# Attention pairs in rounds of two, with the first batch's result kept on chip and the weight decode spread over two rounds

## The chip, the core and the metric

The kernel runs on one NeuronCore of a Trainium2 chip. A core has a matrix engine (PE, TensorE), three elementwise engines (ACT, DVE, POOL), an engine that issues transfers (SP), an on-chip memory SBUF, and PSUM, the memory that PE writes its products to. Each engine works through its own list of instructions; semaphores make one wait for another. The metric is device time in microseconds: 791.69 as the median of three executions (791.29 to 794.2).

## The reference

Three stages follow one another over 4 batches, 448 positions and 768 channels (12 heads of 64):

```
# 1. attention with a sigmoid in place of the softmax
scores = q @ k.T / sqrt(64) - log(448)
x = sigmoid(scores) @ v                      # heads side by side: (4, 448, 768)
# 2. a gated projection
gate = sigmoid(causal depthwise convolution of x, 5 taps, conv_w)
x2 = (gate * (x @ w_val)) @ w_out
# 3. a mixer over positions, then one over channels
u = x2 + (relu(x2.T @ w_tok1) @ w_tok2).T
out = u + relu(u @ w_ch1) @ w_ch2            # hidden width 1536
```

The inputs of stages 2 and 3 need more accuracy than one fast product has, so each 128-channel operand is held as a high and a low part and multiplied three times. Weights arrive as 64-bit words.

## The kernel before

Work is laid out with channels on the partitions. Two heads make a *pair*, so there are 6 pairs per batch and 24 in all, numbered 0 to 23.

**A pair.** `load_qk` and `load_v` fetch q, k and v. `scores(i, c)` multiplies a chunk `c` of 128 keys by all queries for both heads into a PSUM tile `pss`, and `sigmoid` on ACT turns it into a tile `a`. The last 64 keys of two neighbouring pairs share one tile (`scores_last`, PSUM `psl`, SBUF `al`). `av` multiplies the three sigmoid tiles by v into `psy`; `av_last` adds the shared one for both pairs of two, and ACT copies the two results out of PSUM as `x`, which SP stores to a scratch tensor `xscr` in DRAM. `x_back` later loads it again with four zero columns in front (`xb`).

**Per pair, after attention.** `post_parts` computes the convolution `gate` on DVE (one multiply and four multiply-adds) and splits `xb` into `xs`, a high part by ACT and a low part by DVE. ACT's sigmoid over `gate` comes last.

**Decoding a weight.** `fetch` loads a block of 64-bit words into `raw` (three buffers). `decode_parts` gives four steps: `masks` (three DVE instructions), `rebase` (ACT), `low` (three DVE instructions, the last writes the low part) and `high` (ACT writes the high part). There are 18 blocks ahead of the channel mixer: six of `w_val`, six of `w_out`, four of `w_tok1` (`wt1`) and two of `w_tok2` (`wt2`).

**Dense work.** `dense_steps(b)` is a list of steps for one batch: 18 thirds of the `w_val` product (PSUM `psd`, from `xs`), whose results are multiplied by `gate` and split into `gv`, then the `w_out` product (`psd` from `gv`), copied out by ACT as `x2T`, transposed (`pst`), and the mixer over positions (`pst1`, `pst2`). `x2T` lies in a pool `late` that takes over the room of the decode pool `dec`, so its first write waits until the last decode is through.

**What sets the order.** `PLAN` (L25) says which pairs run beside which dense work. Its first two rows are written out by hand in `lead` (pairs 0 to 11, no dense work) and `lead_val` (three pairs beside the `w_val` product of batch 0), inside `manual_schedule`: engines take instructions as they are emitted. From then on a planner sets the order by its own costs; it may also put later instructions between those of the written part, as it does with the convolutions of batch 1. In `lead`, each pair is emitted as `av(i)`, then the scores of pair i+1. `DEC_LEAD` names the eight pairs beside which a block is decoded, `DEC_VAL` spreads seven more over the six half steps of `lead_val`, and the last three are decoded by `late()`. The convolutions of batch 0 start at pair 6 (`POST_FROM`). The channel mixer (`psh`, `pso`) at the end is one dense run of PE.

Of the kernel before, what the change touches and what calls it, by code (L numbers as in the profile page):

```python
# [33 lines left out]
DEC_LEAD = (0, 1, 2, 3, 4, 5, 8, 10)  # L34
DEC_VAL = (1, 1, 1, 1, 1, 2)
CONV_AT = 3

POST_FROM = 6
# [3 lines left out]
def tile_kernel(ctx, tc, qT, kT, v, w_val, conv_w, w_out, w_tok1, w_tok2, w_ch1, w_ch2, out):  # L42
# [63 lines left out]
    def decode_parts(pool, n, raw, h_out, l_out):  # L106
        w = raw[:, : 2 * n].rearrange("p (n t) -> p n t", t=2)
        lo, hi = w[:, :, 0], w[:, :, 1]
        e = raw[:, :n]
        t = {}  # L110

        def masks():
            a = pool.tile([P, DC], I32, tag="dec_a", bufs=2, name="dec_a")[:, :n]
            c = pool.tile([P, DC], I32, tag="dec_c", bufs=1, name="dec_c")[:, :n]
            t["a"], t["c"] = a, c
# [3 lines left out]
                out=c.bitcast(F32), in0=lo.bitcast(U32), scalar=2.0**-32, in1=c, op0=ALU.mult, op1=ALU.add  # L119
# [5 lines left out]
        def low():  # L125
            a, c = t["a"], t["c"]
# [5 lines left out]
                out=l_out, in0=c.bitcast(F32), scalar=2.0**-20, in1=e.bitcast(F32), op0=ALU.mult, op1=ALU.mult  # L132
            )

        def high():
            nc.scalar.activation(out=h_out, in_=t["a"].bitcast(F32), func=AF.Copy)  # L136
# [28 lines left out]
    def dec_conv(pool):  # L165
        n = KD * KW

        def go(raw):
            h = pool.tile([P, n], F32R, tag="cwHL", bufs=1, name="cwH")
            lo = pool.tile([P, n], F32R, tag="cwL", bufs=1, name="cwL")  # L170
            masks, rebase, low, high = decode_parts(pool, n, raw, h, lo)

            def total():
                high()
                nc.vector.tensor_tensor(out=cw, in0=f(h), in1=f(lo), op=ALU.add)

            return masks, rebase, low, total

        return (lambda raw: nc.gpsimd.dma_start(raw, conv_w.bitcast(I32))), go
# [55 lines left out]
    def sigmoid(ps, tag, bufs):  # L235
        a = attn.tile([P, 2, S], F32, tag=tag, bufs=bufs, name=tag)
# [3 lines left out]
    def scores(i, c):  # L240
# [5 lines left out]
        a_t[i, c] = sigmoid(ps, "a", A_BUFS)  # L246
# [22 lines left out]
    def av_last(i):  # L269
# [6 lines left out]
        for h in range(2):  # L276
            x = attn.tile([P, S], F32, tag="x", bufs=2, name="x")
            nc.scalar.activation(out=x, in_=y_t.pop(i + h)[:, :S], func=AF.Copy)
            nc.sync.dma_start(xscr[i + h], x)

    def step_av(i):
        av(i)
        if i % 2:
            av_last(i - 1)
            posts.extend((i - 1, i))
# [16 lines left out]
    def x_back(i):  # L302
        x = attn.tile([P, PAD + S], F32, tag="xb", bufs=2, name="xb")
# [4 lines left out]
    def post_parts(i):  # L308
# [6 lines left out]
        def first():  # L315
# [3 lines left out]
            split(xs[:, 0], xs[:, 1], x[:, PAD:])  # L319
# [5 lines left out]

        def last():
            nc.scalar.activation(out=acc, in_=acc, func=AF.Sigmoid)

        return first, last
# [8 lines left out]
    def dense_steps(b):  # L338
# [3 lines left out]
        def proj(sel, j, part):  # L342
# [16 lines left out]
            if sel == 0:  # L359
                g = gate_t.pop(b * NP + j)  # L360

                def gated():
                    nc.vector.tensor_tensor(out=g, in0=ps[:, :S], in1=g, op=ALU.mult)  # L363
                    gv[j] = mid.tile([P, 2, S], F32R, tag="g", bufs=6, name="gv")
                    split(gv[j][:, 0], gv[j][:, 1], g)

                if dn.get("hold") is None:
                    gated()
                else:
                    dn["hold"].append(gated)  # L370
# [93 lines left out]

    for i in range(2):
        load_qk(i)
    for i in range(2):
        load_v(i)
    load_vl(0)
    load_qk(2)  # L470
    make_identity(nc, ident)
    craw = dec.tile([P, 2 * KD * KW], I32, tag="craw", bufs=1, name="craw")
    cld, cgo = dec_conv(dec)
# [3 lines left out]
    back = 0  # L477
# [32 lines left out]

    def lead():
        nonlocal back
        after = []

        def dec_begin():
            raw, go = raws.pop(0)
            return go(raw)

        dec_load()
        for c in range(NF):  # L520
            scores(0, c)
        scores_last(0)
        dec_load()
        for i in pairs0:
            load_qk(i + 3)
            step_av(i)
            step_loads(i)
            for half in step_scores(i):
                for fn in half:
                    fn()  # L530
# [255 lines left out]
```

## Time and profile before

| | |
|---|---|
| median of three executions | 791.69 us |
| the profiled execution | 795.41 us, span 793.6 us |
| mean granted PE clock | 0.993 of full speed |
| busy: PE / DVE / ACT / POOL | 765.4 / 382.5 / 268.3 / 27.3 us |
| scores of a chunk, L245 (288 records) | 70.5 us, 590 ns mean |
| sigmoid of a chunk, L237 (72) | 69.1 us, 1004 ns mean |
| products with v, L266 (288 records) | 65.7 us, 552 ns mean |
| convolution tap, L321 (96) | 65.1 us, 682 ns mean |
| DMA moved | 80.49 MB, 101 GB/s over the span |

A profiled span of 793.6 us lies inside an execution of 795.41 us. PE is busy for 96% of the span, so what counts is where it is not, and where it is busy for longer than the same work needs elsewhere. In a timeline row the first number is the start, the second the time to the end of the last of `xN` instructions of one kind; records of PE overlap, so the time that a piece of work takes is read from its start to the start of the next piece. A bracket at the end of a row is the idle time before it and what ended it. Products of fp32 operands show two records per instruction.

### The profile page before, as it was taken

What the parts mean: (1) busy time and instruction counts of PE and PEld (TensorE: products, weight loads), DVE (VectorE), ACT (ScalarE), POOL (GpSimd) and SP (SyncE); (2) the same over time, 40 slices, a digit from 0 to 9 for tenths busy, and PEclk for the clock granted to TensorE, in tenths of its full rate; (3) what the DMA queues carried; (4) which work ended last, traced back from release to release, by engine and by line L of the source; (5) the groups of instructions that cost most, each with busy time, mean ns of one, the idle gap of its engine ahead of it and who ended that gap; (6) DMA issues with size and microseconds to landing.
All of it is one profiled execution on the core that took longest, in us unless ns stands there. A gap on an engine that the chain in (4) does not pass through costs nothing.

```text
span 793.6 us, 9619 instructions
## 1 busy us (share of the span) xinstructions
PE 765.4 (96%) x3776; PEld 605.2 (76%) x3776; DVE 382.5 (48%) x659; ACT 268.3 (34%) x404; POOL 27.3 (3%) x73
## 2 busy tenths in 40 slices
PE   7999899699999999999999999999999999999998
PEld 3333456576767777868998999889999999999997
DVE  2758789812583237246688799970002200120002
ACT  5888656523343324232343344430002000100000
POOL 0100001000000000001000000000000000000000
PEclk9999999899999999999999999999999999999999
DMA  8867544312221021014453445551001400050001
GB/s 283 286 231 240 187 149 128 98 33 95 67 84 48 22 72 36 12 47 138 131 191 115 151 163 161 167 192 48 0 1 59 152 1 0 8 190 1 0 1 70
DMA packets 50685, 80.49 MB, mean 101 GB/s; under 512 B 4544, under 2 KB 46032, under 8 KB 50640
## 3 DMA queue, kind: packets, MB, share of 16 engines
q1 hardware_dynamic: 47280, 65.29, 25.8%
q0 software_dynamic: 3360, 14.58, 5.4%
q8 instruction: 30, 0.49, 0.3%
q14 instruction: 15, 0.12, 0.0%
HBM read 63.34 MB, written 16.52 MB: 101 GB/s over the span
## 4 chain that ended last, share of the span: by engine, by line
PE 59%; issue 19%; DVE 12%; DMA 6%; ACT 2%; POOL 1%; SPq 0%; POOLq 0%; DVEq 0%; ACTq 0%
PE psh L675 18%; PE pso L691 18%; PE psd L353 8%; PE psy L266 5%; PE pss L245 5%; DVE gate L321 3%; PE pst L399 2%; DVE dec_a L127 2%; DMA raw<-w_ch 2%; PE pst L412 2%; DVE dec_c L118 2%; DMA k<-kT 1%; ACT a L237 1%; DVE wch L131 1%; DMA xb<-xscr 1%
## 5 line engine op out<-in xcount | busy, mean ns | idle before, releaser
L675 PE MATMUL psh<-us,wch 128*128 128x448 f32 x864 | 184.8, 366 | 0.8 <-ACT wch L136 0.7
L691 PE MATMUL pso<-r,wch 128*128 128x448 f32 x864 | 184.1, 366 | 0.6 <-ACT r L91 0.6
L675 PEld LDWEIGHTS psh<-us,wch 128*128 128x128 f32 x864 | 162.1, 188 | 15.9 <-ACT wch L136 1.7
L691 PEld LDWEIGHTS pso<-r,wch 128*128 128x128 f32 x864 | 162.1, 188 | 15.0 <-ACT r L91 1.0
L93 DVE SCALAR_TENSOR_TENSOR r<-psh,r 128x448 fp32r<-128x448 f32 x48 | 29.9, 624 | 210.3 <-ACT r L91 210.0
L91 ACT ACTIVATE r<-psh 128x448 fp32r<-128x448 f32 x48 | 26.1, 543 | 225.3 <-PE psh L675 225.0
L353 PE MATMUL psd<-gv,w 128*128 128x448 f32 x432 | 96.2, 376 | 1.8 <-DVE gate L363 1.2
L353 PEld LDWEIGHTS psd<-gv,w 128*128 128x128 f32 x432 | 81.1, 192 | 18.7 <-ACT x L384 4.8
L353 PE MATMUL psd<-xs,w 128*128 128x448 f32 x432 | 92.6, 369 | 1.4 <-DVE h L93 1.3
L353 PEld LDWEIGHTS psd<-xs,w 128*128 128x128 f32 x432 | 80.1, 188 | 16.3 <-issue 5.2
L237 ACT ACTIVATE a<-pss,bias_s 128x896 f32<-128x896 f32 x72 | 69.1, 1004 | 34.5 <-PE pss L245 34.2
L245 PE MATMUL pss<-q,k 64*128 64x448 f32 x288 | 70.5, 590 | 4.0 <-DMA k<-kT 4.0
L266 PE MATMUL psy<-a,v 128*64 128x448 f32 x288 | 65.7, 552 | 4.7 <-ACT a L237 4.5
L321 DVE SCALAR_TENSOR_TENSOR gate<-xb,cw,gate 128x448 f32<-128x448 f32 x96 | 65.1, 682 | 1.9
L123 ACT ACTIVATE dec_a<-dec_a,exp_b 128x768 int32<-128x768 int32 (+3 forms) x43 | 37.5, 872 | 59.0 <-DVE dec_a L116 54.4
L245 PEld LDWEIGHTS pss<-q,k 64*128 64x128 f32 x288 | 27.1, 195 | 38.7 <-issue 24.7
L266 PEld LDWEIGHTS psy<-a,v 128*64 128x64 f32 x288 | 18.4, 135 | 41.1 <-ACT a L237 24.0
L127 DVE SCALAR_TENSOR_TENSOR dec_a<-raw,dec_a 128x768 int32<-128x768 int32 (+2 forms) x42 | 37.3, 888 | 11.6 <-ACT dec_a L123 11.5
L118 DVE SCALAR_TENSOR_TENSOR dec_c<-raw,dec_c 128x768 f32<-128x768 uint32 (+2 forms) x42 | 37.4, 890 | 1.0
L374 DVE COPY x2T<-x2T 128x64 f32<-128x64 f32 x24 | 4.5, 192 | 62.8 <-ACT x2T L373 62.8
L116 DVE TENSOR_SCALAR dec_a<-raw 128x768 int32<-128x768 int32 (+2 forms) x42 | 21.9, 521 | 22.5 <-DMA raw<-w_val 13.0
L399 PE MATMUL pst<-x,wt1H 128*128 128x384 f32 x112 | 30.2, 338 | 0.5 <-DVE x L385 0.4
(68 smaller groups left out, 569.3 us busy)
## 6 DMA issues: line engine op xcount, KB each, us to landing
raw<-w_ch SPq DMA_DIRECT2D x24, 768.0 KB, 4.4
q<-qT SPq DMA_DIRECT2D x24, 224.0 KB, 3.3
k<-kT SPq DMA_DIRECT2D x24, 224.0 KB, 4.2
xscr<-x SPq DMA_DIRECT2D x24, 224.0 KB, 2.4
xb<-xscr SPq DMA_DIRECT2D x24, 224.0 KB, 2.6
uscr<-x2T POOLq DMA_DIRECT2D x24, 224.0 KB, 2.4
u<-uscr SPq DMA_DIRECT2D x24, 224.0 KB, 3.6
ur<-uscr SPq DMA_DIRECT2D x24, 224.0 KB, 3.5
```

Of the source, the lines that this page charges most:

```text
L93: nc.vector.scalar_tensor_tensor(out=l_out, in0=src, scalar=0.0, in1=f(h_out), op0=ALU.max, op1=ALU.subtract)
L118: nc.vector.scalar_tensor_tensor(out=c.bitcast(F32), in0=lo.bitcast(U32), scalar=2.0**-32, in1=c, op0=ALU.mult, op1=ALU.add)
L123: nc.scalar.activation(out=t["a"], in_=t["a"], func=AF.Relu, scale=8.0, bias=exp_b)
L127: nc.vector.scalar_tensor_tensor(out=a, in0=hi, scalar=-0x80000000, in1=a, op0=ALU.bitwise_and, op1=ALU.bitwise_or)
L237: nc.scalar.activation(out=a, in_=ps[:, :, :S], func=AF.Sigmoid, bias=bias_s, scale=QK_SCALE)
L245: nc.tensor.matmul(ps[:, j, :S], k[rows, c * P : (c + 1) * P], q[rows], start=True, stop=True)
L266: nc.tensor.matmul(y[cols, :S], vn[:, c, cols], a[:, j], start=c == 0, stop=False)
L321: nc.vector.scalar_tensor_tensor(out=acc, in0=x[:, t : t + S], scalar=cw[:, p * KW + t : p * KW + t + 1], in1=acc, op0=ALU.mult, op1=ALU.add,)
L353: nc.tensor.matmul(ps[:, :S], w(a, kk), s[:, c, :], start=kk == 0 and n == 0, stop=kk == KD - 1 and n == 2,)
L399: nc.tensor.matmul(ps[:, :HALF], a, x[:, m], start=n == 0, stop=n == len(mm) - 1)
L675: nc.tensor.matmul(ps[:, :S], wch[fc][:, 0, a, kk * P : (kk + 1) * P], us_t[b, kk][:, c, :], start=kk == 0 and n == 0, stop=kk == KD - 1 a ...
L691: nc.tensor.matmul(acc[j][:, :S], wch[fc][:, 1, a, j * P : (j + 1) * P], r[:, c, :], start=fc == 0 and n == 0, stop=fc == KF - 1 and n == 2,)
```

## The change

Four things are changed, all in front of the planner's part or in the tables it reads.

- `lead` goes in rounds of two pairs: both `av`, `av_last`, both copies, then all scores of the *next* two pairs. The sigmoid tiles of the round ahead lie in the six buffers of `g`, which `gv` uses later. A second copy out of PSUM is DVE's.
- x of batch 0 (pairs 0 to 5) is written into `xb` with its zero columns and stays there; `xscr` is used from pair 6 on. `xb` now has four buffers, which the copies and `x_back` share; the two buffers of `x` are gone.
- A block's `masks` are emitted one round (in `lead_val` one half step) ahead of its `low` and `high`; the round's `xs` parts and gates likewise follow one and two rounds behind the convolution. `masks` keeps its third result in `raw`, so that `dec_c` is free at once. The small block of `conv_w` is loaded first of all.
- `lead_val` runs beside four pairs (12 to 15), with all remaining ten blocks in `DEC_VAL`; later rows of `PLAN` move by one, and batch 2 runs beside two pairs.

```diff
 PLAN = (
     (None, "", range(0, 12)),
-    (0, "v", range(12, 15)),
-    (0, "o", range(15, 18)),
-    (1, "vo", range(18, 21)),
-    (2, "vo", range(21, 24)),
+    (0, "v", range(12, 16)),
+    (0, "o", range(16, 19)),
+    (1, "vo", range(19, 22)),
+    (2, "vo", range(22, 24)),
     (3, "v", ()),
 )
-DEC_LEAD = (0, 1, 2, 3, 4, 5, 8, 10)
-DEC_VAL = (1, 1, 1, 1, 1, 2)
+DEC_LEAD = (1, 1, 1, 1, 1, 2, 1)
+DEC_VAL = (1, 1, 1, 1, 1, 1, 2, 2)
...
+    def evict(i, on_vector=False, stays=False):
+        y = y_t.pop(i)[:, :S]
+        t = attn.tile([P, PAD + S], F32, tag="xb", bufs=4, name="xb")
+        x = t[:, PAD:]
+        if stays:
+            nc.vector.memset(t[:, :PAD], 0.0)
+            x_t[i] = t
+        if on_vector:
+            nc.vector.tensor_copy(x, y)
+        else:
+            nc.scalar.activation(out=x, in_=y, func=AF.Copy)
+        if not stays:
+            nc.sync.dma_start(xscr[i], x)
+            posts.append(i)
...
+    def dec_masks(n):
+        for _ in range(n):
+            raw, go = raws.pop(0)
+            begun.append((go(raw), True))
+            begun[-1][0][0]()
...
+        dec_masks(DEC_LEAD[0])
+        conved, gates = [], []
+        for n, p in enumerate(pairs0[::2]):
+            done = begun[:]
+            begun.clear()
+            for parts, _ in done:
+                parts[1]()
+            for parts in conved:
+                parts[1]()
+            for parts, _ in done:
+                parts[2]()
                 dec_load()
+            for parts in conved:
+                parts[2]()
+            for fn in gates:
+                fn()
+            for parts, _ in done:
+                parts[3]()
+            gates = [parts[3] for parts in conved]
+            dec_masks(DEC_LEAD[n + 1])
+            for i in (p, p + 1):
+                av(i)
+                load_v(i + 2)
+            av_last(p)
+            load_vl(p + 2)
+            for i in (p, p + 1):
+                evict(i, i > p, p < NP)
+            conved = [post_parts(i) for i in (p, p + 1)] if p < NP else []
+            scores_last(p + 2)
+            for i in (p + 2, p + 3):
+                for c in range(NF):
+                    if i <= pairs0[-1] + 1:
+                        scores(i, c, i <= pairs0[-1])
+                if i + 3 <= pairs0[-1] + 3:
+                    load_qk(i + 3)
+            for parts in conved:
+                parts[0]()
...
 # lead_val, one half step
                 for fn in steps[done:last]:
                     fn()
                 done = last
+                for parts in held:
+                    parts[0]()
+                for fn in subs:
+                    fn()
+                dec_low()
+                dec_masks(DEC_VAL[at])
+                for fn in gates:
+                    fn()
+                for parts in held:
+                    parts[1]()
+                dec_act()
```

PE in the lead, before, over two pairs (`psy` the products with v, `psl` and `pss` the scores):

```order
L266 MATMUL psy<-a,v 64x448 x6
L245 MATMUL pss<-q,k 128x448 x6
L266 MATMUL psy<-a,v 64x448 x6
L275 MATMUL psy<-al,vl 64x448 x4
L256 MATMUL psl<-q,k 64x448 x4
L245 MATMUL pss<-q,k 128x448 x6
```

And one round of the change:

```order
L261 MATMUL psy<-ga,v 64x448 x12
L270 MATMUL psy<-al,vl 64x448 x4
L251 MATMUL psl<-q,k 64x448 x4
L240 MATMUL pss<-q,k 128x448 x12
L261 MATMUL psy<-ga,v 64x448 x12
```

The same instructions stand in fewer, longer blocks: every product with v now has the scores of a whole round between its sigmoid and itself.

ACT in the change, the fourth round, from the end of the third round's sigmoids (`dec_a` is a block's rebase, `w0_3_0` its high part, `xs` and `gate` those of batch 0, `xb` the copy out of PSUM):

```order
L119 ACTIVATE dec_a_438<-dec_a_438,exp_b_66 128x768
L333 ACTIVATE xs_474<-xb_468 128x448
L333 ACTIVATE xs_476<-xb_471 128x448
L339 ACTIVATE gate_366<-gate_366 128x448
L339 ACTIVATE gate_368<-gate_368 128x448
L136 ACTIVATE w0_3_0_98<-dec_a_438 128x768
L282 ACTIVATE xb_577<-psy_552 128x448
L232 ACTIVATE al_588<-psl_583,bias_s_62 128x896
L232 ACTIVATE ga_593<-pss_590,bias_s_62 128x896
```

Six instructions stand between the last sigmoid of one round and the copy that opens the next.

DVE in the change near the end of `lead_val` (`raw_1041` and `raw_1075` are the last two blocks of `w_tok1`, `xb_1256` is x of pair 6 come back from DRAM, `gate_475` and `gv_1062` belong to the projection of batch 0):

```order
L114 SCALAR_TENSOR_TENSOR raw_1041<-raw_1041,dec_c_1144 128x256
L323 TENSOR_SCALAR gate_1263<-xb_1256,cw_69 128x448
L327 SCALAR_TENSOR_TENSOR gate_1263<-xb_1256,cw_69,gate_1263 128x448
L336 TENSOR_TENSOR xs_1262<-xb_1256,xs_1262 128x448
L327 SCALAR_TENSOR_TENSOR gate_1263<-xb_1256,cw_69,gate_1263 128x448
L112 TENSOR_SCALAR dec_a_1148<-raw_1075 128x256
L113 TENSOR_SCALAR dec_c_1149<-raw_1075 128x256
L327 SCALAR_TENSOR_TENSOR gate_1263<-xb_1256,cw_69,gate_1263 128x448
L114 SCALAR_TENSOR_TENSOR raw_1075<-raw_1075,dec_c_1149 128x256
L377 TENSOR_TENSOR gate_475<-psd_1063,gate_475 128x448
```

The planner has put the convolution of pair 6 (batch 1) in front of the last decodes and of the gated products; before, such convolutions stood among the last decodes too. Counted from the first of these `xb_1256` rows, `gv_1135`, the fifth of six `gv`, is the 33rd DVE instruction, and the last row of `wt2` the 43rd.

SP at the same place (`xscr<-xb` stores a pair, `xb<-xscr` loads one back):

```order
L209 DMA k<-kT 128x448
L284 DMA xscr<-xb 128x448
L312 DMA xb<-xscr 128x448
L284 DMA xscr<-xb 128x448
L218 DMA v<-v 128x3x128
L224 DMA vl<-v 64x128 x2
L312 DMA xb<-xscr 128x448 x3
```

The first load of batch 1 stands behind the store of pair 14, which waits for ACT's copy of that pair.

## Rows read from the trace of the kernel before

**Rows 1.** Timeline of PE, two pairs of the lead: start us, us, what.
```profile
9.27 2.48 PE L266 MATMUL psy<-a,v 128*64 128x448 f32 x12
...
16.57 0.98 PE L275 MATMUL psy<-al,vl 64*64 64x448 f32 x8
17.37 0.93 PE L256 MATMUL psl<-q,k 64*64 64x448 f32 x8
18.23 2.53 PE L245 MATMUL pss<-q,k 64*128 64x448 f32 x12
20.69 2.50 PE L266 MATMUL psy<-a,v 128*64 128x448 f32 x12
```

**Rows 2.** Timeline of PE, end of the lead and a projection.
```profile
81.71 0.97 PE L256 MATMUL psl<-q,k 64*64 64x448 f32 x4 [1.91 <-DMA k<-kT]
82.61 4.22 PE L245 MATMUL pss<-q,k 64*128 64x448 f32 x12
88.00 2.48 PE L266 MATMUL psy<-a,v 128*64 128x448 f32 x12 [1.17 <-ACT a L237]
...
96.89 3.91 PE L353 MATMUL psd<-xs,w 128*128 128x448 f32 x18
```

**Rows 3.** Timeline of PE, start of the w_out product.
```profile
141.77 1.77 PE L245 MATMUL pss<-q,k 64*128 64x448 f32 x8
149.80 1.09 PE L382 MATMUL pst<-ident,x2T 128*128 128x128 f32 x4 [6.26 <-issue]
150.54 5.77 PE L353 MATMUL psd<-gv,w 128*128 128x448 f32 x18
```

**Rows 4.** Timeline of DVE and of ACT at the same place.
```profile
143.13 0.68 DVE L321 SCALAR_TENSOR_TENSOR gate<-xb,cw,gate 128x448 f32<-128x448 f32 x1
...
148.38 0.62 DVE L131 SCALAR_TENSOR_TENSOR wt2L<-dec_c,raw 128x448 fp32r<-128x448 f32 x1
...
149.16 0.98 ACT L373 ACTIVATE x2T<-psd 128x448 f32<-128x448 f32 x2 [0.75 <-DVE wt2L L131]
```

**Rows 5.** Windows: length, busy us (instructions) by engine, PE clock, DMA, GB/s.
```profile
80.00:90.00 10.00, 7.12 (x28) 2.69 (x28) 6.05 (x11) 6.75 (x10) 0.73 (x2) 0.83 0.87 292
```

**Rows 6.** Timeline of ACT in the lead.
```profile
65.37 0.94 ACT L123 ACTIVATE dec_a<-dec_a,exp_b 128x768 int32<-128x768 int32 x1
66.21 0.56 ACT L327 ACTIVATE gate<-gate 128x448 f32<-128x448 f32 x1
...
67.65 0.98 ACT L278 ACTIVATE x<-psy 128x448 f32<-128x448 f32 x2 [0.41 <-PE psy L275]
...
69.43 2.80 ACT L237 ACTIVATE a<-pss,bias_s 128x896 f32<-128x896 f32 x3
```

**Rows 7.** Timeline of DVE in the lead: a decode, then a convolution.
```profile
64.78 0.55 DVE L116 TENSOR_SCALAR dec_a<-raw 128x768 int32<-128x768 int32 x1
...
66.72 0.97 DVE L127 SCALAR_TENSOR_TENSOR dec_a<-raw,dec_a 128x768 int32<-128x768 int32 x1
...
69.20 0.45 DVE L316 TENSOR_SCALAR gate<-xb,cw 128x448 f32<-128x448 f32 x1
69.56 0.62 DVE L97 TENSOR_TENSOR xs<-xb,xs 128x448 fp32r<-128x448 f32 x1
70.10 2.84 DVE L321 SCALAR_TENSOR_TENSOR gate<-xb,cw,gate 128x448 f32<-128x448 f32 x4
72.85 0.45 DVE L316 TENSOR_SCALAR gate<-xb,cw 128x448 f32<-128x448 f32 x1
```

**Rows 8.** Groups by line and form, 120 to 150 us: busy us, mean ns.
```profile
L118 DVE SCALAR_TENSOR_TENSOR dec_c<-raw,dec_c 128x256 f32<-128x256 uint32 x4 | 1.7, 422 | 0.1
```

**Rows 9.** DMA issues: queue, count, KB each, median us from issue to landing.
```profile
xb<-xscr SPq DMA_DIRECT2D x24, 224.0 KB, 2.6
...
raw<-w_val SPq DMA_DIRECT2D x3, 768.0 KB, 7.1
raw<-w_val POOLq DMA_DIRECT2D x3, 768.0 KB, 5.8
raw<-w_tok POOLq DMA_DIRECT2D x2, 448.0 KB, 5.5
```

More of the change, by code (lines that the diff above doesn't have):

```diff
@@ L168, in go @@
         def go(raw):
[L169 to L177, printed above, removed]
+            return decode_parts(pool, n, raw, None, pool.tile([P, n], F32, tag="cwL", bufs=1, name="cwL"), cw)
         return (lambda raw: nc.gpsimd.dma_start(raw, conv_w.bitcast(I32))), go
@@ L324, in first, with high, low @@
                 )
+        def high():
+            nc.scalar.activation(out=xs[:, 0], in_=x[:, PAD:], func=AF.Copy)
+        def low():
+            nc.vector.tensor_tensor(out=xs[:, 1], in0=x[:, PAD:], in1=f(xs[:, 0]), op=ALU.subtract)
         def last():
             nc.scalar.activation(out=acc, in_=acc, func=AF.Sigmoid)
-        return first, last
+        return conv, high, low, last
     def post_pair(i):
@@ L463, in dec_go @@
             dec_load()
+    craw = dec.tile([P, 2 * KD * KW], I32, tag="craw", bufs=1, name="craw")
+    cld, cgo = dec_conv(dec)
+    cld(craw)
     for i in range(2):
         load_qk(i)
[L467 to L470, printed above, removed]
     make_identity(nc, ident)
-    craw = dec.tile([P, 2 * KD * KW], I32, tag="craw", bufs=1, name="craw")
-    cld, cgo = dec_conv(dec)
     pend, posts = [], []
@@ L507, in tile_kernel, with dec_low, dec_act @@
     pairs0 = PLAN[0][2]
-    def lead():
[L512 to L517, printed above, removed]
+    begun, going = [], []
+    def dec_masks(n):
[3 more added lines that the diff above has]
+            begun[-1][0][0]()
+    def dec_low():
+        for parts, loads in going:
+            parts[2]()
+            if loads:
+                dec_load()
+    def dec_act():
+        for parts, _ in going:
+            parts[3]()
+        for parts, _ in begun:
+            parts[1]()
+        going[:] = begun
+        begun.clear()
@@ L519, in lead @@
+    def lead():
+        dec_load()
+        for i in range(2):
+            load_v(i)
+        load_vl(0)
+        load_qk(2)
         dec_load()
         for c in range(NF):
-            scores(0, c)
+            scores(0, c, True)
+        for part in cgo(craw):
+            part()
         scores_last(0)
+        load_qk(3)
+        for c in range(NF):
+            scores(1, c, True)
+        load_qk(4)
         dec_load()
[L524 to L530, printed above, removed]
-            behind, after = after, []
-            if i in DEC_LEAD:
-                masks, rebase, low, high = dec_begin()
-                masks()
-                rebase()
-                for fn in behind:
-                    fn()
-                low()
-                after.append(high)
-                dec_load()
-            else:
-                for fn in behind:
-                    fn()
-            if i == CONV_AT - 1:
-                cld(craw)
-            if i == CONV_AT:
-                for part in cgo(craw):
-                    part()
-            if i >= POST_FROM and posts[0] < NP:
-                first, last = post_parts(posts.pop(0))
-                first()
-                after.append(last)
-            if i + 1 >= POST_FROM and back < NP:
-                x_back(back)
-                back += 1
@@ L560, in lead_val @@
+        assert not (conved or gates)
+        dec_act()
+    def lead_val(steps, pairs):
+        subs, gates = [], []
         slots = 2 * len(pairs)
-        todo = [n for n in DEC_VAL]
         hold = dn["hold"] = []
@@ L601, in tile_kernel @@
         rest_of[0] = None, steps[nval:]
-        lead_val(after, [fn for _, fn in steps[:nval]], PLAN[1][2])
+        lead_val([fn for _, fn in steps[:nval]], PLAN[1][2])
         mark(0)
```

90 lines of the change are left out of this document (47 added, 43 removed).

## The prediction

> **What bounds the kernel now.** I read the summary of busy time first: PE is busy nearly all the time, so a change can only win where PE waits, or where its work takes longer than the same work elsewhere. Then I read PE's timeline from the start to the channel mixer, looking for the brackets, and the windows for the clock.
>
> In the lead PE repeats one pattern [rows 1]. Two pairs take 20.69 - 9.27 = 11.42 us: two products with v, the shared ones (0.80, from 16.57 to 17.37), the shared scores (0.86), and twice 2.46 us of scores (18.23 to 20.69). That leaves (11.42 - 0.80 - 0.86 - 4.92) / 2 = 2.42 us for one product with v. These pieces follow one another without a gap where nothing is late, so 11.42 us is what a round of two pairs costs on PE.
>
> The lead is longer than that. Its end is the row at 88.00, the first product with v of pair 12 [rows 2]. In front of it stand three kinds of loss: PE waited 1.91 us for a transfer of k; the scores that followed took 4.22 us in place of 2.46; and it waited for a sigmoid, 1.17 us there. [...] The kernel has no reserve here: a product with v is emitted one pair after its scores, and ACT does decode work in between.
>
> The second place is the start of the `w_out` product [rows 3]. PE ends a score at 143.54, stands for 6.26 us, and its next `w_out` third takes 5.77 us in place of 3.91 (the `w_val` row of the same size in [rows 2]), again after an idle stretch: 6.26 + 1.86 = 8.1 us. The views of ACT and DVE name the cause [rows 4]: the copy `x2T` waited for the last `wt2L`, the end of the decode, whose room `x2T` takes.
>
> **The change, part by part.**
>
> *The lead in rounds.* It removes no PE work. The first scores start as before, on the same transfers, so the first product with v, at 9.27 before, moves behind the scores of pair 1: 9.27 + 2.46 = 11.73. Six rounds follow; the last has the scores of one pair only: 11.73 + 5 x 11.42 + (11.42 - 2.46) = 77.8 us for the product of pair 12, if PE never waits. Against 88.00 that is 10.2 us. The question is what could be late in a round, counted from its start T.
>
> ACT: the last sigmoids of the round before, then a rebase, two `xs`, two gates, a `high`, the copy, and `al`. A sigmoid takes 2.80 / 3 = 0.93 us, a rebase 0.94, an `xs` or a gate 0.56, a copy 0.98 / 2 = 0.49 [rows 6]; a `high` I take like a rebase. In a full round that is 7 x 0.93 + 2 x 0.94 + 4 x 0.56 + 0.49 = 11.1 us, under 11.42. Started at T + 6.5 (the end of the shared scores), the sigmoids end at T + 13.0, which is 1.6 us into the next round; the six others follow until 5.7, and the copy can begin at 5.64. So ACT is just in time.
>
> DVE: a decode takes 69.20 - 64.78 = 4.42 us, a convolution with its low part 72.85 - 69.20 = 3.65, of which 0.54 the low part [rows 7]. The copy out of PSUM on DVE is new. The same copy on ACT takes 0.49 [rows 6], a tap over as many columns 0.68 [rows 4]; I take 0.6, near the tap, the nearest row of its own engine, and the ends differ by 0.2 us a round. Together 4.42 + 7.3 + 0.6 = 12.3 us in the rounds with everything, 0.9 over PE's 11.42, and there are two such rounds. [...] In round 0 the convolutions start after the copies, near T + 7.4, and end at 7.4 + 6.2 = 13.6, 2.2 us into round 1. They end 3.1 us into round 2 and 4.0 into round 3. There DVE's first instruction of `low` (0.97) ends at 5.0, `high` on ACT at 5.9, the copy at 6.4, and `al` is wanted at 6.5. From round 3 on there are no convolutions and DVE catches up. So nothing is late, with 0.1 us to spare in one round. Bounds: a loss of 0 to 5 us (all six rounds at DVE's 12.3). I take 0.
>
> Transfers: twelve of 224 KB, the stores and loads of batch 0, leave SP's queue. In a round, q and k are asked for when their buffer comes free at T + 9 and are wanted at T + 17, so the 7.1 us of the slowest kind of load [rows 9] still fits. The wait of 1.91 us for k goes.
>
> *`lead_val` with four pairs.* PE's work is the same, in another split; the sum of both stages doesn't change. From 77.8 to the end of the shared product of pair 15 there are four products with v, three times scores, two shared ones, one shared score, and 78 of the 108 projection instructions (4.33 x 3.91): 9.7 + 7.4 + 1.6 + 0.9 + 16.9 = 36.5, which is 114.3 us.
>
> *The end of the decode.* Here the order works against the intent: the decode doesn't end beside the four pairs. DVE's list has the convolution of pair 6 in front of the last decodes, and SP loads that pair back only behind the store of pair 14, so behind ACT's copy at 114.3. With 0.49 for the copy and 2.6 for the load [rows 6, 9], DVE goes on at 117.5 at the earliest; before that it has only 2 us of work after 110 (its product for j=3) and then stands still. From there 15 instructions lead to the one that frees the buffer for the last block of `w_tok2`: nine at (148.38 - 143.13) / 11 = 0.48 [rows 4] and six of 256 columns at 0.42 [rows 8], 6.8 us: 124.3. That block lands 5.5 us later [rows 9], at 129.8 (DVE reaches it at 128.5, after 6 x 0.48 + 3 x 0.42). Nine more instructions, 4.3 us, end with `gv_1135`: 134.1.
>
> PE wants `gv_1135` after a shared score, scores of pair 16, 30 projection instructions, the product of pair 16, two thirds of the scores of pair 17 and 12 `w_out` instructions: 114.3 + 0.86 + 2.46 + 6.5 + 2.42 + 1.64 + 2.6 = 130.8. So PE waits 3.3 us. The last `wt2L` comes ten instructions later, 138.9, and PE needs `x2T` only at 134.1 + 1.3 + 3.9 + 0.8 = 140.1: no second wait. Standing still for 1.91 us cost PE 4.22 - 2.46 = 1.76 us at the lower clock afterwards [rows 2, 5]; I add 1.8, with 0 to 1.9 as bounds [rows 3]. So 5.1 in place of 8.1 us: 3.0 won. Bounds: 8.1 won (no wait) to 2 lost.
>
> [...] POOL issues the blocks that DVE waits for. The row: `w_val` blocks of 768 KB took 7.1 us from SP's queue and 5.8 from POOL's, beside a decoding DVE [rows 9]. [...]
>
> *The rest.* The planner's part has the same work with the pairs one later; PE's list there is alike. I take 0, between 2 us lost (batch 2 has two pairs, not three, to fill with) and 2 won.
>
> **Sum.** 10.2 + 3.0 = 13.2 us. The profiled execution took 795.4, its span 793.6; that execution is 3.7 us over the median of 791.7, so from the median 791.7 - 13.2 = 778.5 us. I say 778.
>
> **Rivals.**
>
> *The tail clears too.* If the load of pair 6 comes early enough or the planner's order costs nothing, both waits go: 791.7 - 10.2 - 8.1 = 773.4. For it: DVE has 5 us to spare just before. Against: the order of SP's and DVE's lists.
>
> *DVE sets the rounds.* If instructions on ACT and DVE don't close up as in [rows 6, 7], the excess of 0.9 us shows in each of six rounds: 778.5 + 5.4 = 784. For it: the 0.1 us of reserve. Against: three rounds carry no convolution.
>
> *The decode ends as late as before.* The lead's gain stays, the tail's 8.1 us too: 791.7 - 10.2 = 781.5, or some more. For it: the chain load, convolution, free buffer, load, decode has two transfers in a row.
>
> *Slower.* If `al` is late by 1.9 us in each round, PE stands there as it did for k, and the clock falls afterwards: 1.91 + 1.76 = 3.7 us a round [rows 2], 22 in six, 778.5 + 22 = 800. It decides from 13.2 / 6 = 2.2 us a round. For it: a round's shared pieces are where PE stood at 81.71 when the clock fell. Against: ACT's sum is below PE's.
>
> **Chances.** Forecast 0.52 (own range 775 to 782), tail clears 0.12, DVE sets the rounds 0.14, decode as late 0.15, slower 0.07. The range 772 to 787 leaves out the slower case and the outer parts of the others. A difference of under 0.5% (4 us) can't be told from none. Faster by more: the first four cases but for 0.01 of the third and 0.05 of the fourth, 0.87; same 0.06; slower 0.07.
>
> **What would show it.** Right: the first product of pair 12 near 78 us; no bracket over 0.5 us in the rounds; a `psd<-gv` row with a bracket near 3 us ended by DVE or ACT, not a `pst` row with 6; DVE idle for some 4 us before `gate<-xb` at 117. Wrong: brackets at `psl` or `psy` in each round, or a lower granted clock before 78 us (the lead's step); a `pst` row still waiting for `wt2L` (the tail's); more waiting between 200 and 440 us (the rest).

## The result and the profile after

| | before | changed |
|---|---|---|
| median of four executions | 792.55 us | 784.07 us |
| the profiled execution, its span | 795.41, 793.6 us | 784.53, 782.8 us |
| mean granted PE clock there | 0.993 | 0.997 |
| DMA moved | 80.49 MB | 77.73 MB |

The ratio is 0.989, with a 95% interval of 0.9865 to 0.9915: 8.5 us faster, where 13.2 were forecast. Where the time went is read from PE's two timelines; all three stages end at the first `psh` row.

| stretch of PE | forecast | the two traces |
|---|---|---|
| up to the first product of pair 12 | -10.2 | 88.00 to 79.44: -8.6 |
| start of `w_out`: waits and work at the lower clock | -3.0 | 0.54 + 6.26 + 1.86 to 1.18 + 0.20 + 1.40 + 1.47 + 1.60: -2.8 |
| waits of 0.18 us or more from 230 to 430 us | 0 | 5.2 to 6.9: +1.6 |
| not attributed | | -1.0 |
| first `psh` | | 426.45 to 415.73: -10.7 |

The medians differ by 2.2 us less than the first `psh` rows, because the profiled execution of before lies 2.9 us above its median and the changed one's 0.5; the other 0.2 us lie behind these rows.

PE's timeline in the changed kernel, the first round, the fourth and the last (start, length, what; in brackets the idle time before a row), as an answer to [rows 1, 2]:

```profile
11.34 4.73 PE L261 MATMUL psy<-ga,v 128*64 128x448 f32 x24
...
17.66 4.98 PE L240 MATMUL pss<-q,k 64*128 64x448 f32 x24
22.57 4.73 PE L261 MATMUL psy<-ga,v 128*64 128x448 f32 x24
...
45.10 4.73 PE L261 MATMUL psy<-ga,v 128*64 128x448 f32 x24
...
51.42 1.77 PE L240 MATMUL pss<-q,k 64*128 64x448 f32 x8
53.59 3.72 PE L240 MATMUL pss<-q,k 64*128 64x448 f32 x16 [0.39 <-ACT al L232]
57.24 4.73 PE L261 MATMUL psy<-ga,v 128*64 128x448 f32 x24
...
68.50 4.73 PE L261 MATMUL psy<-ga,v 128*64 128x448 f32 x24
...
74.83 2.94 PE L240 MATMUL pss<-q,k 64*128 64x448 f32 x12
79.44 2.48 PE L261 MATMUL psy<-a,v 128*64 128x448 f32 x12 [1.67 <-ACT a L232]
```

A round takes 22.57 - 11.34 = 11.23 us, without a gap. The fourth takes 57.24 - 45.10 = 12.14, and the product of pair 12 waits 1.67 us. ACT shows what stood in front of `al` both times (the answer to [rows 6]):

```profile
51.36 0.85 ACT L136 ACTIVATE w<-dec_a 128x768 fp32r<-128x768 f32 x1 [1.89 <-DVE dec_a L124]
52.11 0.53 ACT L282 ACTIVATE xb<-psy 128x448 f32<-128x448 f32 x1
52.54 1.00 ACT L232 ACTIVATE al<-psl,bias_s 128x896 f32<-128x896 f32 x1
...
74.52 0.84 ACT L136 ACTIVATE w<-dec_a 128x768 fp32r<-128x768 f32 x1 [1.61 <-DVE dec_a L124]
75.27 0.53 ACT L282 ACTIVATE xb<-psy 128x448 f32<-128x448 f32 x1
75.69 1.00 ACT L232 ACTIVATE al<-psl,bias_s 128x896 f32<-128x896 f32 x1
76.58 2.81 ACT L232 ACTIVATE a<-pss,bias_s 128x896 f32<-128x896 f32 x3
```

The block's `high` waits for DVE's `low`, and the copy and `al`, which wait for nothing of DVE's, are queued behind it. In the fourth round DVE is late: the convolutions of the third come first. In the last round there is none; two blocks are decoded, and DVE stands for 4.32 us until ACT, behind the sigmoids, has done the first rebase. DVE's copy out of PSUM takes 0.63 us (the answer to [rows 7]):

```profile
43.33 0.63 DVE L280 COPY xb<-psy 128x448 f32<-128x448 f32 x1
...
47.60 2.85 DVE L327 SCALAR_TENSOR_TENSOR gate<-xb,cw,gate 128x448 f32<-128x448 f32 x4
50.36 0.96 DVE L124 SCALAR_TENSOR_TENSOR dec_a<-raw,dec_a 128x768 int32<-128x768 int32 x1
...
71.05 0.98 DVE L124 SCALAR_TENSOR_TENSOR dec_a<-raw,dec_a 128x768 int32<-128x768 int32 x1 [4.32 <-ACT dec_a L119]
```

The start of the `w_out` product, PE and then DVE (the answer to [rows 3, 4]):

```profile
130.90 3.11 PE L365 MATMUL psd<-gv,w 128*128 128x448 f32 x14
135.19 4.73 PE L365 MATMUL psd<-gv,w 128*128 128x448 f32 x22 [1.18 <-DVE gv L383]
...
146.76 0.63 PE L401 MATMUL pst<-ident,x2T 128*128 128x128 f32 x4 [1.40 <-DVE x L405]
...
160.19 5.51 PE L365 MATMUL psd<-gv,w 128*128 128x448 f32 x18 [1.47 <-ACT x2T L392]
```

```profile
114.36 0.43 DVE L114 SCALAR_TENSOR_TENSOR raw<-raw,dec_c 128x256 f32<-128x256 uint32 x1
120.54 0.45 DVE L323 TENSOR_SCALAR gate<-xb,cw 128x448 f32<-128x448 f32 x1 [5.76 <-DMA xb<-xscr]
...
139.62 0.64 DVE L128 SCALAR_TENSOR_TENSOR wt2L<-raw,dec_e 128x448 fp32r<-128x448 f32 x1
...
143.34 2.50 DVE L327 SCALAR_TENSOR_TENSOR gate<-xb,cw,gate 128x448 f32<-128x448 f32 x4
145.72 0.58 DVE L404 TENSOR_TENSOR x<-pst,x 128x384 fp32r<-128x384 f32 x1
```

The one stall of 6.26 us has become four short ones (1.18, 0.20, 1.40 and 1.47). The wait of 1.40 us is for L404 and L405, the low part of a transposed tile, and convolution taps of batch 1 stand in front of them. DVE stands for x of pair 6, as forecast, though for 5.76 us until 120.5 and not for some 4 until 117; the instruction in front of it is the one of [rows 8], 0.43 us again. The windows (length, busy time by engine, then PE clock) show the lower clock gone from 80 to 90 us, against [rows 5], and back behind the wait at 160:

```profile
80.00:90.00 10.00, 10.00 (x50) 5.98 (x48) 7.83 (x12) 5.84 (x8) 1.48 (x2) 1.00 0.74 254
155.00:165.00 10.00, 8.53 (x34) 6.92 (x33) 5.04 (x10) 3.53 (x6) 0.00 (x0) 0.83 0.25 80
```

Of the transfers of [rows 9], the last column is the median from issue to landing:

```profile
xb<-xscr SPq DMA_DIRECT2D x18, 224.0 KB, 2.8
raw<-w_tok POOLq DMA_DIRECT2D x2, 448.0 KB, 3.5
```

### The profile page after: what moved, and what is told of

It reads as the page before. It is cut to its first block, busy times and chain, and to the rows that moved or that the text cites. A ratio compares the mean times of both kernels' runs of the same rounds, so it can differ in the third digit from the quotient of the medians.

```text
span 782.8 us, 9546 instructions
## 1 busy us (share of the span) xinstructions
PE 760.2 (97%) x3776; PEld 604.0 (77%) x3776; DVE 385.1 (49%) x671; ACT 264.2 (34%) x397; POOL 26.9 (3%) x67
## 2 busy tenths in 40 slices
DMA packets 48957, 77.73 MB, mean 99 GB/s; under 512 B 4352, under 2 KB 44304, under 8 KB 48912
## 4 chain that ended last, share of the span: by engine, by line
PE 64%; DVE 15%; issue 13%; DMA 3%; ACT 3%; POOL 1%; SPq 0%; POOLq 0%; DVEq 0%; ACTq 0%
PE psh L734 18%; PE pso L750 18%; PE psd L365 13%; PE psy L261 5%; PE pss L240 4%; DVE gate L327 4%; DVE dec_a L124 2%; PE pst L431 2%; DVE raw L114 2%; PE pst L418 1%; DMA xb<-xscr 1%; DVE wch L128 1%; DVE dec_e L127 1%; DVE dec_a L112 1%; DVE dec_c L113 1%
## 5 line engine op out<-in xcount | busy, mean ns | idle before, releaser
L240 PE MATMUL pss<-q,k 64*128 64x448 f32 x288 | 68.8, 578 | 4.7 <-DMA k<-kT 4.1
L232 ACT ACTIVATE a<-pss,bias_s 128x896 f32<-128x896 f32 x36 | 35.0, 1006 | 24.0 <-PE pss L240 21.3
L114 DVE SCALAR_TENSOR_TENSOR raw<-raw,dec_c 128x768 f32<-128x768 uint32 (+2 forms) x42 | 37.6, 895 | 1.2
L261 PE MATMUL psy<-a,v 128*64 128x448 f32 x144 | 34.0, 550 | 1.7 <-ACT a L232 1.7
L232 ACT ACTIVATE ga<-pss,bias_s 128x896 f32<-128x896 f32 x36 | 33.2, 1019 | 4.1 <-PE pss L240 4.1
L377 DVE TENSOR_TENSOR gate<-psd,gate 128x448 f32<-128x448 f32 x24 | 15.0, 623 | 39.6 <-PE psd L365 39.5
L136 ACT ACTIVATE wch<-dec_a 128x768 fp32r<-128x768 f32 x24 | 20.3, 846 | 29.6 <-DVE dec_a L124 22.5
```

Source lines behind the costliest of these rows:

```text
L114: nc.vector.scalar_tensor_tensor(out=lo.bitcast(F32), in0=lo.bitcast(U32), scalar=2.0**-32, in1=c, op0=ALU.mult, op1=ALU.add)
L232: nc.scalar.activation(out=a, in_=ps[:, :, :S], func=AF.Sigmoid, bias=bias_s, scale=QK_SCALE)
L240: nc.tensor.matmul(ps[:, j, :S], k[rows, c * P : (c + 1) * P], q[rows], start=True, stop=True)
L261: nc.tensor.matmul(y[cols, :S], vn[:, c, cols], a[:, j], start=c == 0, stop=False)
```

## The experiments

**The changed kernel again**, on the chip of two later runs.

> The changed kernel as it is, on the same chip as the two runs beside it, so that these can be compared with it and not with a number from another chip. All theories: a ratio to the kernel before of 0.989, some 784 us.

783.89 us, ratio 0.9887 (0.9868 to 0.9906). This is what the runs below are held against.

### The two halves of the change

**Rounds without the new stages.** The changed kernel with `PLAN` of before and `DEC_VAL = (1, 1, 1, 1, 1, 2)`; the last three blocks are decoded in `late()`.

> The changed kernel with the stages' table of the kernel before: lead_val beside three pairs, seven decodes in it, the last three by late(). The lead stays in rounds. Theory (of the whole gain the lead brings some 8.6 us, the placement of the decode the rest): the first product of pair 12 stays at 79.4 us, and the w_out product again meets a stall like the 6.26 + 1.86 us of the kernel before; in the changed kernel the same place costs 1.2 + 1.4 us of waits and 1.5 + 1.6 further on, so this kernel is 784.1 + 2.4 = 786.5 us (785 to 788). Rival, the placement is worth nothing by itself, because what waits is only moved: 784. Rival, the placement is most of the gain: 790 or more.

786.44 us, 0.9912 (0.9883 to 0.994). Pair 12 starts at 79.63. The stall is back, 4.98 us, and the row behind it takes 5.74 us for 18 instructions in place of 3.91:

```profile
138.88 1.32 PE L401 MATMUL pst<-ident,x2T 128*128 128x128 f32 x4 [4.98 <-issue]
139.85 5.74 PE L365 MATMUL psd<-gv,w 128*128 128x448 f32 x18
```

The lead brings most of the gain. The 2.0 us that the placement adds lie inside the two intervals.

**The tables alone.** The kernel before with the new `PLAN` and `DEC_VAL = (1, 1, 1, 1, 1, 1, 2, 2)`.

> The kernel before with only the changed tables: four pairs in lead_val with the last ten decodes, three, three and two pairs behind. The lead is as before. Theory: the lead's waits stay, the first product of pair 12 at 88 us, and only the tail's 2.4 us are won: 792.5 - 2.4 = 790 us (788 to 793). Here x_back has buffers of its own, so the convolution of pair 6 shouldn't make DVE stand for 5.8 us; if that stall is the price of the shared xb buffers, the tail clears and this kernel wins 5 to 8 us: 785 to 787. Rival, masks not a half step ahead make the decode end as late: 792.5.

788.53 us, 0.993 (0.9902 to 0.9957): 5.4 us, more than expected, though the tail doesn't clear (4.48 us of waiting for `gv`, and the 21 `w_out` instructions behind it take 7.29 us, where 22 take 4.73 in the changed kernel). Part of it isn't the edit's: in the lead, which is that of before, PE waits longer for k than in [rows 2] and the clock stays up (a granted clock of 1.00 from 80 to 90 us).

```profile
81.07 0.97 PE L256 MATMUL psl<-q,k 64*64 64x448 f32 x4 [2.39 <-DMA k<-kT]
...
85.96 2.48 PE L266 MATMUL psy<-a,v 128*64 128x448 f32 x12 [1.46 <-ACT a L237]
```

From the shared score to pair 12 it is 85.96 - 81.07 = 4.89 us here, 88.00 - 81.71 = 6.29 in [rows 2]. From the first product to pair 12 the same lead takes 85.96 - 9.96 = 76.0 us here, 88.00 - 9.27 = 78.7 in the trace of before. Both halves together (7.5 + 5.4) would be more than the whole change's 8.8; how much of them is the same time stays open.

**x of batch 0 by way of DRAM.** Only the second part is undone:

```diff
-                evict(i, i > p, p < NP)
+                evict(i, i > p)
+            if p < NP:
+                posts.clear()
+                for i in (p, p + 1):
+                    x_back(i)
```

> The changed kernel without its second part: x of batch 0 goes through the scratch tensor again (store, then load by x_back in the same round), the rounds and tables stay. Theory (in a round ACT's copy and al stand behind high, and high behind DVE's convolutions): a convolution can begin only after store and load, some 5 us later than the 7.4 us into its round, so it ends 7 us into the next round, high comes at 10 us, and PE waits for al or psy some 3 to 5 us in each of the rounds 1 to 3 (and near 1 in the fourth): the first product of pair 12 at 88 to 95 us in place of 79.4, and 784.1 + 9 to + 15 us, 793 to 799: the lead's gain is lost. Rival, x on chip only saves transfers, which are hidden: 784 to 786.

801.18 us, 1.0091 (1.0062 to 1.0121): slower than before. PE and ACT in the second round:

```profile
30.32 0.97 PE L251 MATMUL psl<-q,k 64*64 64x448 f32 x4 [1.29 <-DMA k<-kT]
...
36.68 5.12 PE L240 MATMUL pss<-q,k 64*128 64x448 f32 x16 [3.69 <-ACT al L232]
```

```profile
34.45 0.84 ACT L136 ACTIVATE w<-dec_a 128x768 fp32r<-128x768 f32 x1 [6.35 <-DVE dec_a L124]
35.20 0.53 ACT L282 ACTIVATE xb<-psy 128x448 f32<-128x448 f32 x1
35.62 1.00 ACT L232 ACTIVATE al<-psl,bias_s 128x896 f32<-128x896 f32 x1
```

The traced execution took 796.36 us, the shortest of the four. The chain is the expected one, and k is late too, since q and k stand behind the loads of x in SP's list (issued from 25.37 us on, the loads of x at 24.35); how much of the loss either brings, the run doesn't separate. With the loads in this place the rounds lose more than they win, so x on the chip is worth far more than the 2.8 MB of transfers that it saves.

### The lead

**`high` between the sigmoids.**

```diff
-            for parts, _ in done:
-                parts[3]()
...
             for i in (p + 2, p + 3):
+                if i > p + 2:
+                    for parts, _ in done:
+                        parts[3]()
                 for c in range(NF):
...
-DEC_LEAD = (1, 1, 1, 1, 1, 2, 1)
-DEC_VAL = (1, 1, 1, 1, 1, 1, 2, 2)
+DEC_LEAD = (1, 1, 1, 1, 1, 1, 1)
+DEC_VAL = (1, 1, 1, 2, 1, 1, 2, 2)
```

> In the changed kernel ACT's high of a block moves from in front of the copy and the shared sigmoid to between the two pairs' sigmoids, and no round has two decodes: one of w_out moves to the fourth half step of lead_val. Theory (the lead fell short because high waits for DVE's low with copy and al queued behind it: 0.39 + 0.5 us in the fourth round, 1.67 in the sixth): both brackets go, the first product of pair 12 starts at 77.8 us in place of 79.44 (77 to 78.2), and the time is 784.1 - 2 = 782 us (781 to 783). Rival, DVE itself is what is late, and its copy out of PSUM behind the masks takes the place of al: brackets on psy instead, 784. Rival, the decode moved into lead_val makes the tail later: the lead wins 2, the tail loses it again, 784.

782.62 us, 0.9853 (0.9825 to 0.9882). All full rounds are now free of gaps, 11.26 us each (12.79 to 69.10 in five). In the fourth this is the place of `high` alone; in the last the edit also takes one of two decodes away, so what either does there isn't told apart. But pair 12 still waits 1.43 us, with neither `high` nor DVE in front:

```profile
79.39 2.48 PE L261 MATMUL psy<-a,v 128*64 128x448 f32 x12 [1.43 <-ACT a L232]
```

```profile
76.53 2.80 ACT L232 ACTIVATE a<-pss,bias_s 128x896 f32<-128x896 f32 x3
```

The product starts when the third sigmoid is through (79.33), though its first instructions read the first sigmoid only. From the first product on, the lead is 79.39 - 12.79 = 66.6 us, 1.5 less than the changed kernel's 68.1; its start at 12.79 is a later one, since the first twelve scores took 4.85 us, not 3.90, and the shared ones behind them 1.64, not 0.98.

**Scores of pair 12 a round ahead.** On top of that edit: `scores(12, c)` behind those of pair 11, and both copies of the last round on ACT.

> The run with high between the sigmoids, with one edit more: the scores of pair 12 also come a round ahead (their sigmoid tiles are the three buffers of a), and the last round copies both results on ACT. Theory (pair 12's product waits not for its own sigmoids but for all readers of the score tiles: behind it a new PSUM pool takes over, and its first instruction waits for ACT's last read of the old one): its sigmoids are done a round before, and PE waits all the same, now for al, some 1.1 us (shared score 0.9 us, then al 0.9 to 1.0). Rival (it waits for its own sigmoids, which aren't a round ahead there): no bracket at that row; it follows the shared score at once. Times: 782.6 - 0.4 = 782.2 us by the first, 782.6 - 1.4 = 781.2 by the second.

```profile
79.75 2.48 PE L261 MATMUL psy<-a,v 128*64 128x448 f32 x12 [1.21 <-ACT al L232]
```

```profile
71.00 2.84 ACT L232 ACTIVATE a<-pss,bias_s 128x896 f32<-128x896 f32 x3
...
78.69 1.01 ACT L232 ACTIVATE al<-psl,bias_s 128x896 f32<-128x896 f32 x1
```

Pair 12's sigmoids were done at 73.8, and PE waits until `al` at 79.7, which this product doesn't read. In both runs it starts when ACT's last read of the lead's score tiles is through. In the kernel this product is the first use of a new PSUM pool (`psl` released, `psa` taken), which is taken for the reason. Whether it waits for the whole old pool, or only for the room that it takes over, stays open: the last score tile lies in the same one of three buffers in both runs. The time, 785.07 us (0.9893, 0.9875 to 0.9911), isn't better. From the first product on the lead is 79.75 - 12.42 = 67.3 us, 0.7 longer than with the one edit: ACT had three more sigmoids in the round before, and PE waited 0.61 us for one there.

**Both copies on ACT** (`evict(i, False, p < NP)`).

> The changed kernel with both copies out of PSUM on ACT; DVE's copy, which the trace after shows at 0.63 us, goes. Theory (ACT has slack in a round: al is wanted only when the third score tile needs its buffer, and it comes 1 us before that): rounds without a bracket stay at 11.26 us; in the fourth and the last round DVE's low comes 0.6 us earlier and ACT's copies take 0.43 longer, so these waits stay within 0.3 us: 784.1 +- 0.7. Rival, the forecast's sum (ACT is just in time at 11.1 of 11.42 us): 0.43 us in each of four rounds, 785.8 or more.

785.43 us, 0.9904 (0.9881 to 0.9926). Rounds one to three take 11.25 to 11.28 us, the fourth 12.07; the only new wait is 0.55 us for `al` in the last. DVE's copy is worth about nothing in the full rounds; the two intervals overlap.

### The tail

**Convolutions of batch 1 from pair 17 on.** In the planner's row of the first `w_out` product:

```diff
-            post(2)
+            if b or n:
+                post(2)
...
-            post(2)
+            if b or n:
+                post(2)
```

> In the changed kernel the loads and convolutions of batch 1 are emitted from pair 17 on, not from pair 16. Theory (DVE stood 5.76 us for x of pair 6, queued in front of the last decodes): DVE goes on with the last blocks of w_tok at 115 us, the last wt2L comes by 132 us in place of 140.3, the waits of 1.18 us before the fifth third of w_out and 1.40 us before the second transposition go, and perhaps the 1.47 + 1.6 at 160 us: 784.1 - 2.6 to 784.1 - 5.7, 778.4 to 781.5 us. Rival, the convolutions are only owed: they meet the projection of batch 1 from 196 us on and PE waits there for xs or gate, 784 or more. Rival, PE doesn't wait for the decode there but for gv's own copies: 784.

781.02 us, 0.9832 (0.9805 to 0.9858). The waits of 1.18, 0.20 and 1.40 us are gone, the one for `x2T` is left. But DVE stands nearly as long as before, 5.50 us:

```profile
130.76 7.57 PE L365 MATMUL psd<-gv,w 128*128 128x448 f32 x36
...
156.79 5.48 PE L365 MATMUL psd<-gv,w 128*128 128x448 f32 x18 [1.50 <-ACT x2T L392]
```

```profile
120.48 0.29 DVE L112 TENSOR_SCALAR dec_a<-raw 128x256 int32<-128x256 int32 x1 [5.50 <-ACT wt1H L136]
```

So the stand had two causes at the same time: x of pair 6, and the second of two mask buffers, which ACT's `high` frees only behind the copy of pairs 14 and 15 (at 120.01, the copy at 116.89). Taking the first away shortened nothing; what was won came from the convolutions that no longer stand between the decodes and in front of `gv` and of L404. The rest, `x2T`, stands behind `xs` on ACT, which waits for a load of x:

```profile
155.02 1.29 ACT L333 ACTIVATE xs<-xb 128x448 fp32r<-128x448 f32 x2 [2.63 <-DMA xb<-xscr]
156.21 0.53 ACT L392 ACTIVATE x2T<-psd 128x448 f32<-128x448 f32 x1
```

**Loads of batch 1 issued by POOL.** In `x_back`, `(nc.gpsimd if i < 2 * NP else nc.sync).dma_start(...)`.

> The changed kernel with one edit: the loads of x of batch 1 (xb<-xscr of pairs 6 to 11) are issued by POOL, which already writes their zero columns, and no longer by SP behind the store of pair 14. Theory (the convolution of pair 6 comes late through the order of SP's list): POOL issues the first load at 114.8 us, where its zero columns stand now, x lands near 117.5, and DVE stands some 2 us, not 5.76; ACT's xs doesn't wait 1.88 us in front of a sigmoid. PE's waits of 1.18 us before the w_out product and of 1.47 us at 160 us (with 1.6 us at the lower clock behind it) become smaller or go: 784.1 - 1.5 to 784.1 - 4.3, 780 to 782.6 us. Rival, from the run with the later convolutions, where DVE stood 5.50 us at the same place for ACT's high of the block before: the second mask buffer holds DVE there whatever x does, and the 33 instructions in front of gv are as many: 783.5 to 784.5. Rival, loads issued by POOL land later beside a busy DVE: 785 or more.

782.05 us, 0.9864 (0.9844 to 0.9885), not told apart from the changed kernel. POOL issues the first load at 116.90, DVE goes on at 121.32 after 4.46 us, not some 2, and PE waits 1.58 us for `gv`, no less than before. (All times here lie some 2 us later than in the changed kernel's trace, since the product of pair 12 took 4.15 us in place of 2.48.)

**Loads of pairs 6 and 7 early**, in the fourth half step of `lead_val`, with the edits of `high` and of `post`.

```diff
+                if at == 3:
+                    x_back(NP)
+                    x_back(NP + 1)
+                    back = NP + 2
```

> The changed kernel with high between the sigmoids and the convolutions of batch 1 emitted from pair 17 on, and the loads of pairs 6 and 7 written out in the fourth half step of lead_val, by SP, in front of the stores of pairs 14 and 15. The convolutions of these two then stand among the decodes of w_out in DVE's list, the other four behind the last wt2L. Theory (what decides is where in DVE's and ACT's lists the instructions that wait for x stand): no wait at the start of the w_out product, and the wait for x2T near 156 us, which stood behind xs<-xb in two runs (1.50 and 1.34 us, with 1.6 us at the lower clock), goes, since only four loads are left and the first has its x early: 784.1 - 1.4 - 3.0 - 1.5 to -3, 776.5 to 778.5 us. Rival, DVE hasn't the 7.3 us for two convolutions there (it is idle for 6.5 of 35 us between 80 and 115): gate is late, PE waits for a psd buffer near 105 us, 780 or more. Rival, x of pair 8 is as late as that of pair 6 was, and x2T waits behind it as before: 779.6.

784.51 us, 0.9891 (0.9874 to 0.9909): what the two other edits win is lost again. DVE hasn't the room, as the first rival had it, though it shows not on `psd` but on a sigmoid behind `high`:

```profile
114.67 0.84 ACT L136 ACTIVATE w<-dec_a 128x768 fp32r<-128x768 f32 x1 [2.55 <-DVE dec_a L124]
...
117.59 0.99 ACT L232 ACTIVATE a<-pss,bias_s 128x896 f32<-128x896 f32 x1
```

```profile
118.63 0.97 PE L261 MATMUL psy<-a,v 128*64 128x448 f32 x4 [3.65 <-ACT a L232]
```

**Three edits, two edits.** `high` between the sigmoids and later convolutions, with and without the loads on POOL.

> The changed kernel with three edits at once: high between the two pairs' sigmoids (1.4 us won alone), convolutions of batch 1 from pair 17 on (3.0 won alone), and their loads issued by POOL. Theory: the gains lie in different stages and add up, 784.1 - 1.4 - 3.0 = 779.6, and with the loads on POOL the wait of 1.50 us for x2T behind xs (and 1.6 us at the lower clock) goes as well: 776.5 to 779.6 us. Rival, the edits meet in the same place (the decode's end), and only the larger counts: 781.

> The changed kernel with two edits: high between the sigmoids, and the convolutions of batch 1 emitted from pair 17 on; their loads stay with SP. Theory (the two edits lie in different stages and add, and the POOL queue of the run with three edits added nothing): 784 - 1.4 - 3.0 = 779.6 us, a ratio of 0.9835 to the kernel before, with waits of 1.43 us at pair 12 and 1.3 to 1.5 us for x2T near 156 us left. Rival (the edits meet in the decode's end, and only the later convolutions count): 781. Rival, the POOL queue was worth something: 781.5 or more.

780.29 us, 0.9826 (0.9802 to 0.985), and 780.2 us, 0.9835 (0.9807 to 0.9863). Both beat the changed kernel; the loads on POOL add nothing that can be seen. The later convolutions alone had 0.9832, so `high` adds nothing measurable to them in the median; in the traces the lead is shorter (78.72 - 12.14 = 66.6 us from the first product, against 79.64 - 11.65 = 68.0).

## Why the prediction was right, and where it was short

**A round.** 11.42 us forecast, 11.23 to 11.27 measured in four rounds, no lower clock (a granted clock of 1.00 from 11.34 to 79.44 us), no wait for k: right. DVE's copy out of PSUM, taken at 0.6, took 0.63.

**"Nothing is late, with 0.1 us to spare in one round."** The round was the right one and the mechanism too; the reserve was not there. The convolutions ended 5.3 us into the fourth round (50.36 - 45.10), not 4.0, and the round lost 0.9 us. The edit of `high` took this away.

**"(11.42 - 2.46) = 77.8 us ... if PE never waits."** This step of the lead failed: the last round took 79.44 - 68.50 = 10.94 us, 2.0 more. The sum had counted PE's instructions only. It left out that this product, the first in a new PSUM pool, doesn't start before ACT's last sigmoid of the lead is through; that is 1.43 us (`high` between the sigmoids), with `high` in front 1.67, and 1.21 where pair 12's own sigmoids are early. The rest is scores spread out behind `al` (2.94 us in place of 2.46), because `high` of the second block waited for its `low` there. The wait is shown; that the pool is its cause is read from the kernel.

**The tail.** That DVE would stand for x of pair 6, and that a short wait for `gv` takes the place of the long one, was right, and 2.8 us won against 3.0 looks right. The terms are not, so that the sum came out is luck: the wait is 1.18 us, not 3.3, and no lower clock follows it (1.00 from 133 to 138 us; PE arrives 1.6 us later than reckoned counted from the lead's end, and the blocks of `w_tok2` took 3.5 us in the median, not 5.5). "No second wait" was wrong: 1.40 and 1.47 us, and 1.60 at the lower clock, from instructions of batch 1 that the planner put in front of L404 and of `x2T`.

**POOL's transfers.** The last block of `w_tok2`, which POOL issues, was taken to land after 5.5 us. In the changed kernel it was issued at 127.38 and DVE, without a gap in between, read it at 130.79 without a wait, 3.4 us later. In the run with later convolutions DVE waited 2.11 us for it, but there too it came 4.4 us after its issue (123.94 to 128.37), under the 5.5. In the run with loads on POOL the two blocks took 4.2 us in the median; a load of x took 4.4 us (116.90 to 121.32), but DVE stood idle meanwhile. So no run here shows that a busy DVE makes POOL's transfers land later, as the last rival of that run has it.

**The rest.** Nothing was forecast, within 2 us either way. The traces show 1.6 us more waiting from 230 to 430 us, which by the prediction's own sign makes this step wrong, though within its bounds; no run here looks for the cause. Another 1.0 us, in the other direction, is not attributed.

**From a trace to the median.** The sum was made against an execution 3.7 us above the median and taken from the median whole. That execution had two falls of the clock (0.83 from 80 to 90 us, 0.50 from 150 to 154 behind the stall), and the tables-only run shows the same lead without the first: 1.4 us of the 10.2 are not in every execution. Nor is a wait for a sigmoid further up, which the trace of before has and the tables-only run, the second row, has not:

```profile
52.52 2.48 PE L266 MATMUL psy<-a,v 128*64 128x448 f32 x12 [1.55 <-ACT a L237]
```

```profile
51.61 2.51 PE L266 MATMUL psy<-a,v 128*64 128x448 f32 x12
```

In all, the same lead is 2.7 us shorter there (76.0 against 78.7), so a forecast from one trace of it is uncertain by that much. The clock differs between executions of the changed kernel too: those at a mean clock of 1.000 took 782.84 and 783.61 us, those at 0.997 and 0.996 took 784.53 and 784.63.

**The rivals.** DVE setting the rounds (784) gave the number, but not the mechanism: one round was late through DVE, not six, so its number is luck. The tail didn't clear; the decode didn't end as late as before either, as the stall of 6.26 us is gone. `al` wasn't late in each round; where x goes by DRAM it is late in three of them (3.69, 2.67 and 2.05 us), and that kernel is slower than before, so the slower rival's mechanism exists.

## What to carry to other kernels

In an engine's list look for the instruction that waits for another engine, and at what is queued behind it that doesn't: moving `high` between the sigmoids, with one decode moved out of the lead, made the full rounds free of gaps and cost no time that can be seen. A round's sum held for the middle rounds here (11.23 to 11.27 us against 11.42); the last one (10.94 against 8.96) and the change to a new buffer pool (waits of 1.21 to 1.67 us) want a sum of their own. A long wait can have two causes, and taking one away shows the other, as DVE's stand did (5.76 us, then 5.50): read who ends the wait in the run without the first, before the gain is put down to it.

## What the hardware showed unexpectedly

Whether the clock falls behind a wait of 1.3 to 2.7 us is not told by its length in these traces. Behind the wait of 1.67 us at pair 12, the twelve records of the product took 2.48 us in five traces (a granted clock of 1.00 from 80 to 85 us in that of the changed kernel) and 4.15 and 4.17 in two (loads on POOL; the changed kernel again, with 0.66 from 80 to 85 us):

```profile
80.25 4.17 PE L261 MATMUL psy<-a,v 128*64 128x448 f32 x12 [1.67 <-ACT a L232]
```

Behind the wait for `x2T` near 160 us, 1.34 to 1.64 us long, 18 projection instructions took 5.47 to 5.51 us in five traces and 3.90 to 3.98 in five others (a granted clock from 160 to 165 us of 0.66 in the changed kernel's trace, of 1.00 in that of the changed kernel again). Read from such times, after 1.34 us the clock fell (5.47), after 1.50 it fell in one run (later convolutions, 5.48) and not in another (`high` between the sigmoids, 3.91), and after 2.39 us for k (tables alone, 2.53 us for twelve score records) and 2.67 for `al` (x by DRAM, 3.72 for sixteen) it didn't. Behind the five longer waits that were read it fell each time: after 6.26 and 4.98 us 18 instructions took 5.77 and 5.74, after 4.48 us 21 took 7.29, after 3.69 us sixteen score records took 5.12, and after 3.65 us (loads early) eight of the shared product took 1.77, not 0.98. What decides it for the shorter ones stays open. In a forecast the 1.6 us belong into the range, not into the sum.
